# Forming the distance from the threshold to the largest score on VectorE, beside the selection, in a top-k attention and ELU kernel

## The chip, the cores and the metric

The kernel runs on one core of a Trainium2 chip. The metric is the device time of one execution in microseconds, from a median of several runs. The engines are named as in the profile: PE is the matrix engine (TensorE), PEld its weight loads, DVE is VectorE, ACT is ScalarE, POOL is GpSimd and SP issues DMAs.

## What is computed

The input is q, k and v with 8 batches, 8 heads, 576 rows and 64 columns, and two weights of an ELU layer. The reference, cut to what matters:

```python
scores = scale * np.matmul(q, k.transpose(0, 1, 3, 2))          # 576 x 576 for each head
kth = np.partition(scores, -top_k, axis=-1)[..., -top_k:-top_k + 1]   # top_k = 32
scores = np.where(scores >= kth, scores, -1000000000.0)
scores = scores - np.max(scores, axis=-1, keepdims=True)
attn = np.exp(scores)
attn = attn / (np.sum(attn, axis=-1, keepdims=True) + 1e-09)
o = np.matmul(attn, v)
# heads side by side: x is 4608 x 512
h = x @ w_in                                                    # 512 x 2048
g = np.where(h > 0.0, h, np.exp(np.minimum(h, 0.0)) - 1.0)
out = g @ w_out                                                 # 2048 x 512
```

Each row of scores needs its 32nd largest value (the threshold), its largest value, and the sum of exponentials over the kept scores. The kernel writes the exponential with a bias that is threshold minus largest score: this "gap" is one number for each row.

## The kernel before

**Steps.** The attention is cut into steps. A step is one tile of 128 query rows and two heads, so it handles two "score rows" of 128 partitions by 576 keys (index `i` is 0 or 1). There are 144 steps. In the first 8 (`n < tight`) the weights are still being decoded beside the selection and another form of it is used (`select_row`); three more use `select`; the last 133, from about 157 us on, use `select_folded`, and these are the ones the change touches.

**One step, by engine.** `scores` (L326) makes the scores on PE and ACT copies them from PSUM to SBUF (L343), two steps ahead. `select_folded` (L391) finds the 32nd largest on DVE: it folds a row of 576 into a row `high` of 288 maxima (L402), while POOL forms the 288 minima `low` in two integer operations (L403, L406). DVE takes the 32 largest of `high` by rounds of MAX8 and MATCH_REPLACE8 (L410 to L420), the 16 largest of `low` (L424 to L428), and joins the two lists (L430, L431). L430 writes the minima of pairs over places 15 to 30 of `found`, and L431 reduces them to the threshold, `u.last[:, i, 7]`. The largest score is `found[:, i, 0]`, left as it was by the join.

`mask(u, i)` (L436) belongs to the next step of the loop: for the previous tile, POOL forms the gap of one row (L453, one number for each partition), ACT sets what lies under the threshold far away (L454) and takes the exponential with the gap as its bias and the row sum as a by-product (L455 and the read of the accumulator behind it). `normalise` (L459) forms the reciprocal of the sums on POOL in five small operations (L465 to L470) and multiplies both rows by it (L472, two operations). One loop later `turn` (L476) transposes the rows on PE (L491), ACT copies them to SBUF (L492), and `attend` (L501) multiplies them by v on PE (L517) and copies the result to the layer's input (L544).

**The layer.** `ffn_pieces` (L565) gives pieces of the ELU layer: `hidden` (PE L589, three ACT operations L599, L602 and L604, and a DVE operation L561 that joins the two halves of the ELU, called a gate) and `project` (PE L614, ACT L623, output by DMA). `feed` (L702) places such pieces between the parts of a step, by costs and due times that are fixed when the program is built. So the order on each engine is written out at build time: the engines run it strictly in that order and wait for each other by semaphores.

**The order around the change.** With `cur` the step in selection and `prev` the one before, the loop (L743 to L797) issues in a folded step:

- DVE: L402, L410, rounds of L415 and L420, L424, L426, L428, L430, L431 for `cur`, with gates L561 in between
- POOL: L403 and L406 for `cur`, then L453 twice and L465 to L472 for `prev`
- ACT: L343 for a later step, then for `prev` L454 and L455 of row 0, pieces of the layer, L492 twice for the step before `prev`, L454 and L455 of row 1, pieces, L492 once more
- PE: scores of a later step, L517 of a finished group, pieces of the layer, transposes L491 in three portions with pieces in between

The tile `den` holds four numbers for each partition: two sums and two gaps. It comes from the pool `small`, with four buffers of each kind. `wk`, in which POOL writes `low`, has one buffer.

Of the kernel before, what the change touches and what calls it, by code (L numbers as in the profile page):

```python
# [9 lines left out]
ALU = mybir.AluOpType  # L10
AX = mybir.AxisListType
FP32 = mybir.dt.float32
# [13 lines left out]
class Tile:  # L26
# [6 lines left out]
    def __init__(self, b, qt, rows, block, cols):  # L33
        self.b, self.qt, self.rem = b, qt, qt == 4
        self.rows = rows
        self.block = block
        self.cols = cols
        self.ql = cols.stop - cols.start
# [21 lines left out]
class Step:  # L60
# [7 lines left out]
    def __init__(self, t, hp, group, at):  # L68
        self.t, self.hp = t, hp
        self.group, self.at = group, at  # L70
        self.masked = self.normal = self.turned = False
        if t.rem:
            rows = [(4 * hp, 0), (4 * hp + 2, 0), (4 * hp + 3, 1), (4 * hp + 1, 1)]
            self.heads = [
                (h, i, slice(64 * (n % 2), 64 * (n % 2) + 64))
                for n, (h, i) in enumerate(rows)
            ]
        else:
            self.heads = [(2 * hp + i, i, slice(0, 128)) for i in range(2)]
# [3 lines left out]
def kernel(  # L83
# [9 lines left out]
    nc = tc.nc  # L93
    P = nc.NUM_PARTITIONS
# [18 lines left out]
    def pool(name, bufs, **kw):  # L113
        return ctx.enter_context(tc.tile_pool(name=name, bufs=bufs, **kw))
# [6 lines left out]
    small = pool("small", 4)  # L121
# [269 lines left out]
    def select_folded(u):  # L391

        one, other = u.sc[:, :, 0:HS], u.sc[:, :, HS:S]
        high = late["high"].tile([P, 2, HS], FP32, tag="high", name="high")
        rest, low = (
            wk[:, i, :].rearrange("p (a s) -> p a s", a=2) for i in range(2)
        )
        found = late["top"].tile([P, 2, TOP_K], FP32, tag="found", name="found")
        second = late["top"].tile([P, 2, TOP_K // 2], FP32, tag="second", name="second")
        u.first = found  # L400
        u.last = small.tile([P, 2, 8], FP32, tag="m4", name="m4")
        nc.vector.tensor_tensor(high[:], one, other, ALU.max)  # L402
        nc.gpsimd.tensor_tensor(  # L403
            low.bitcast(I32), one.bitcast(I32), other.bitcast(I32), ALU.add
        )
        nc.gpsimd.tensor_tensor(  # L406
            low.bitcast(I32), low.bitcast(I32), high[:].bitcast(I32), ALU.subtract
        )
        for i in range(2):
            nc.vector.max(found[:, i, 0:8], high[:, i, :])  # L410
        yield
        cur = high
        for r in range(0, TOP_K - 8, 8):
            for i in range(2):
                nc.vector.match_replace(  # L415
                    rest[:, i, :], found[:, i, r : r + 8], cur[:, i, :], TAKEN
                )
            cur = rest
            for i in range(2):
                nc.vector.max(found[:, i, r + 8 : r + 16], rest[:, i, :])  # L420
            if r < TOP_K - 16:
                yield
        for i in range(2):
            nc.vector.max(second[:, i, 0:8], low[:, i, :])  # L424
        for i in range(2):
            nc.vector.match_replace(low[:, i, :], second[:, i, 0:8], low[:, i, :], TAKEN)  # L426
        for i in range(2):
            nc.vector.max(second[:, i, 8:16], low[:, i, :])  # L428
        pairs = found[:, :, TOP_K // 2 - 1 : TOP_K - 1]
        nc.vector.tensor_tensor(pairs, pairs, second[:, :, ::-1], ALU.min)  # L430
        nc.vector.tensor_reduce(  # L431
            u.last[:, :, 7:8], found[:, :, TOP_K // 2 - 1 : TOP_K], AX.X, ALU.max
        )
        yield

    def mask(u, i, early=False):  # L436

        if u.masked:
            return
        if i == 0:
            u.den = small.tile([P, 4], FP32, tag="den", name="den")
        u.masked = i == 1
        sc, low, top = u.sc[:, i, :], u.last[:, i, 7:8], u.first[:, i, 0:1]
        gap = u.den[:, 2 + i : 3 + i]
        if early:  # L450
            nc.scalar.activation(gap, top, AF.Prelu, scale=-1.0, bias=low, alpha=1.0)
        else:
            nc.gpsimd.tensor_tensor(gap, low, top, ALU.subtract)  # L453
        nc.scalar.activation(sc, sc, AF.Prelu, scale=-1.0, bias=low, alpha=1.0 / STEEP)  # L454
        nc.scalar.activation(  # L455
            sc, sc, AF.Exp, scale=-STEEP, bias=gap, accum_out=u.den[:, i : i + 1]
        )
# [285 lines left out]
    for n in range(NS + 3):  # L743
# [3 lines left out]
        if n < tight:  # L747
            turn_qk(True)
            if n < 3:
                scores(ahead)  # L750
            if n > 1:
                scores(step(n + 3))
            for i in range(2):
                passes = select_row(cur, i, n < tight - 1)
                next(passes)
                if i == 0:
                    while closing:
                        attend(closing.pop(0))
                elif prev:
                    normalise(prev)  # L760
                    turn(prev, main)
                    turn(prev, rest)
                    turn(prev, other)
                feed(n, 0.25)
                next(passes)
                mask(cur, i, True)
                feed(n, 0.25)
            continue
# [10 lines left out]
        if prev:  # L779
            mask(prev, 0)  # L780
# [6 lines left out]
        if prev:  # L787
            mask(prev, 1)
# [45 lines left out]
```

## Time and profile before

| | |
|---|---|
| median of 3 runs | 1723.7 us (1722.95 to 1725.91) |
| the profiled execution | 1726.9 us |
| its span, first to last instruction | 1725.1 us |
| PE busy | 1628.8 us, 94% of the span |
| DVE busy | 1456.8 us, 84% |
| ACT busy | 1099.1 us, 64% |
| POOL busy | 970.3 us, 56% |
| L453 on POOL, folded steps | 266 operations, 201 ns mean |
| L430 and L431 on DVE | 133 each, 192 and 191 ns mean |
| clock granted to PE | 0.97 of full speed, mean of the span |

The busy time of an engine is the time in which at least one of its instructions is in progress. A list of waits names the engine and line that sat idle, who ended the idle time, and then the microseconds in total, the number of waits and the longest one. In a timeline each row has the start, the duration, the engine, the line, the operation, its output and inputs, and in brackets the idle time of that engine before it with the one who ended it. A table of stretches gives, for each window of the span, the busy time of each engine with the number of instructions in brackets, then the granted clock of PE, the share of the DMA engines and the bandwidth.

### The profile page before, as it was taken

The numbers are of one execution on the slowest core, as the hardware profiler recorded it, in microseconds if no ns is written. First come the engines' busy times: TensorE is split into PE (matmuls) and PEld (weight loads), VectorE is DVE, ScalarE is ACT, GpSimd is POOL, SyncE is SP. The second block draws the span as 40 slices with busy tenths as digits, with TensorE's granted clock in tenths as the row PEclk, the third lists the DMA queues.
The fourth block names the chain that finished last, engine by engine and source line by source line (L and its number), as shares of the span: only waits on it lengthen the run. The fifth ranks groups of instructions, "written<-read, shape, count | busy, mean of one in ns | idle before, by whom it ended". The sixth has DMA issues, their size and how long they took to land.

```text
span 1725.1 us, 27135 instructions
## 1 busy us (share of the span) xinstructions
PE 1628.8 (94%) x8276; PEld 1029.4 (60%) x8276; DVE 1456.8 (84%) x4587; ACT 1099.1 (64%) x2305; POOL 970.3 (56%) x1681
## 2 busy tenths in 40 slices
PE   5789999999999999999999999999999999999999
PEld 3466667656565656555556565755557565755565
DVE  6978999998998998998988998889988898887600
ACT  6887666666575666666657565667657575666521
POOL 3765666665656566555655655556665556555400
PEclk8579999999999999999999999999999999999999
DMA  7431210012100210011200211002200101000000
GB/s 231 139 111 35 49 34 15 7 21 41 42 1 7 48 34 21 1 27 35 42 13 1 46 23 41 1 7 48 42 13 7 26 15 28 7 7 7 7 13 13
DMA packets 188050, 56.29 MB, mean 33 GB/s; under 512 B 178176, under 2 KB 179200, under 8 KB 187904
## 3 DMA queue, kind: packets, MB, share of 16 engines
q1 hardware_dynamic: 186704, 54.26, 13.5%
q8 instruction: 66, 1.08, 0.3%
q14 instruction: 80, 0.66, 0.1%
q10 hardware_dynamic: 1200, 0.30, 0.1%
HBM read 45.09 MB, written 9.44 MB: 32 GB/s over the span
## 4 chain that ended last, share of the span: by engine, by line
PE 30%; POOL 28%; ACT 21%; DVE 14%; issue 5%; DMA 1%; SPq 0%; POOLq 0%; DVEq 0%; ACTq 0%
PE ops L614 15%; POOL sc L472 7%; ACT sc L455 6%; POOL wk L406 6%; POOL wk L403 6%; PE hps L589 6%; PE avps L517 5%; ACT sc L454 4%; ACT et L492 4%; POOL rec L467 3%; DVE wk L415 3%; PE scps L335 2%; DVE found L420 2%; DVE second L424 2%; PE eps L491 2%
## 5 line engine op out<-in xcount | busy, mean ns | idle before, releaser
L589 PE MATMUL hps<-xT,w_in 128*128 128x256 f32 (+2 forms) x2432 | 548.1, 375 | 0.6 <-ACT gT L602 0.4
L614 PE MATMUL ops<-w_out,gT 128*128 128x512 f32 x1152 | 522.9, 598 | 0.0
L589 PEld LDWEIGHTS hps<-xT,w_in 128*128 128x128 f32 x2432 | 408.4, 194 | 101.8 <-issue 27.7
L455 ACT ACTIVATE sc<-sc,den 128x576 f32<-128x576 f32 x288 | 223.5, 776 | 352.5 <-POOL den L453 337.1
L465 POOL TENSOR_SCALAR dene<-den 128x2 f32<-128x2 f32 x144 | 37.7, 262 | 556.4 <-ACT sc L455 555.9
L614 PEld LDWEIGHTS ops<-w_out,gT 128*128 128x128 f32 x1152 | 208.9, 190 | 233.5 <-issue 213.5
L420 DVE MAX8 found<-wk 128x8 f32<-128x288 f32 x798 | 323.1, 446 | 0.0
L335 PE MATMUL scps<-kqT 64*128 64x288 f32 (+1 forms) x1280 | 226.3, 444 | 35.9 <-ACT et L492 23.3
L517 PE MATMUL avps<-et,vT 128*64 128x256 f32 (+2 forms) x2080 | 228.3, 337 | 30.8 <-ACT et L492 30.1
L472 POOL TENSOR_SCALAR sc<-sc,rec 128x576 f32<-128x576 f32 x288 | 233.6, 821 | 14.9 <-POOL rec L470 0.2
L415 DVE MATCH_REPLACE8 wk<-found,wk 128x288 f32<-128x288 f32 x532 | 231.2, 442 | 0.0
L454 ACT ACTIVATE sc<-sc,m 128x576 f32<-128x576 f32 x288 | 227.0, 788 | 0.0
L517 PEld LDWEIGHTS avps<-et,vT 128*64 128x64 f32 x2080 | 135.9, 145 | 125.0 <-ACT et L492 55.8
L561 DVE SCALAR_TENSOR_TENSOR gT<-n,gT 128x512 f32<-128x512 f32 (+1 forms) x156 | 112.5, 721 | 113.1 <-ACT n L604 113.1
L491 PEld LDWEIGHTS eps<-ident,sc 128*128 128x128 f32 x1152 | 145.1, 145 | 89.5 <-issue 49.7
L406 POOL TENSOR_TENSOR wk<-wk,high 128x576 int32<-128x576 int32 x133 | 190.7, 1434 | 10.4
L335 PEld LDWEIGHTS scps<-kqT 64*128 64x128 f32 (+1 forms) x1280 | 118.8, 182 | 124.9 <-issue 44.8
L491 PE MATMUL eps<-ident,sc 128*128 128x128 f32 x1152 | 177.5, 280 | 15.2 <-POOL sc L472 15.1
L343 ACT ACTIVATE sc<-scps 128x576 f32<-128x576 f32 x288 | 173.4, 657 | 28.9 <-PE scps L335 28.0
L403 POOL TENSOR_TENSOR wk<-sc 128x576 int32<-128x576 int32 x133 | 190.7, 1434 | 0.0
L424 DVE MAX8 second<-wk 128x8 f32<-128x288 f32 x266 | 108.3, 448 | 89.0 <-POOL wk L406 88.9
L492 ACT COPY et<-eps 128x512 f32<-128x512 f32 x288 | 164.8, 572 | 23.7 <-PE eps L491 23.7
(67 smaller groups left out, 1759.2 us busy)
## 6 DMA issues: line engine op xcount, KB each, us to landing
raw<-in_moe_w_in_dram SPq DMA_DIRECT2D x16, 512.0 KB, 5.8
vT<-in_v_dram SPq DMA_DIRECT2D x64, 128.0 KB, 2.4
raw<-in_moe_w_out_dram SPq DMA_DIRECT2D x16, 512.0 KB, 4.0
out_dram<-osb SPq DMA_DIRECT2D x32, 256.0 KB, 2.1
kin<-in_k_dram SPq DMA_DIRECT2D x112, 72.0 KB, 2.4
qin<-in_q_dram SPq DMA_DIRECT2D x112, 72.0 KB, 2.5
kin<-in_k_dram SPq DMA_DIRECT2D x8, 128.0 KB, 4.6
vT<-in_v_dram SPq DMA_DIRECT2D x64, 16.0 KB, 2.2
```

The costliest lines, as they stand in the source:

```text
L335: nc.tensor.matmul(wide[i][rows, half, 0:HS], kq[part, q0 : q0 + u.t.ql], kq[part, k0 : k0 + HS], start=True, stop=True,)
L403: nc.gpsimd.tensor_tensor(low.bitcast(I32), one.bitcast(I32), other.bitcast(I32), ALU.add)
L406: nc.gpsimd.tensor_tensor(low.bitcast(I32), low.bitcast(I32), high[:].bitcast(I32), ALU.subtract)
L415: nc.vector.match_replace(rest[:, i, :], found[:, i, r : r + 8], cur[:, i, :], TAKEN)
L420: nc.vector.max(found[:, i, r + 8 : r + 16], rest[:, i, :])
L454: nc.scalar.activation(sc, sc, AF.Prelu, scale=-1.0, bias=low, alpha=1.0 / STEEP)
L455: nc.scalar.activation(sc, sc, AF.Exp, scale=-STEEP, bias=gap, accum_out=u.den[:, i : i + 1])
L472: nc.gpsimd.tensor_scalar(u.sc[:, i, :], u.sc[:, i, :], rec[:, i : i + 1], 1.0, ALU.mult, ALU.mult)
L491: nc.tensor.transpose(ps[:, c * P : (c + 1) * P], sc[:, c0 : c0 + P], ident[:])
L517: nc.tensor.matmul(ps[i * D : (i + 1) * D, cols], vt[:, 2 * J + i if c == J else i * J + c, :], w, start=(c == 0), stop=(c == J),)
L589: nc.tensor.matmul(blk.h[:, f % bank, :], w_in[:, i, f * P : (f + 1) * P], blk.xT[:, i, 0:n_tok], start=(i == 0), stop=(i == NC - 1),)
L614: nc.tensor.matmul(blk.o[:], blk.gT[f // NG][:, f % NG, s * P : (s + 1) * P], w_out[:, f, :], start=(f == 0), stop=(f == NF - 1),)
```

## The change

In folded steps the gap is formed at the end of `select_folded`, on DVE, right behind the join: one operation on 128 partitions by 2 numbers covers both rows. `den` is therefore allocated there, one loop earlier than before. `mask` no longer forms the gap for such steps; the two POOL operations (L453) are not issued. Steps that are not folded keep what they had. The order of the PE and ACT queues is the same in both programs; DVE's has 133 operations more and POOL's 266 fewer.

```diff
@@ Step.__init__
-        self.masked = self.normal = self.turned = False
+        self.masked = self.normal = self.turned = self.spread = False
+        self.den = None
@@ select_folded
-        u.first = found
+        u.first, u.spread = found, True
...
         nc.vector.tensor_reduce(
             u.last[:, :, 7:8], found[:, :, TOP_K // 2 - 1 : TOP_K], AX.X, ALU.max
         )
+        u.den = small.tile([P, 4], FP32, tag="den", name="den")
+        nc.vector.tensor_tensor(
+            u.den[:, 2:4], u.last[:, :, 7], found[:, :, 0], ALU.subtract
+        )
         yield
@@ mask
-        if i == 0:
+        if u.den is None:
             u.den = small.tile([P, 4], FP32, tag="den", name="den")
...
-        else:
+        elif not u.spread:
             nc.gpsimd.tensor_tensor(gap, low, top, ALU.subtract)
```

## The prediction

> **What bounds the kernel now.** I read the list of waits first. Three of its rows form a ring:
>
> ```profile
> POOL dene L465 <- ACT sc L455: 555.9, 139, 10.8
> ACT sc L455 <- POOL den L453: 337.1, 106, 5.4
> DVE second L424 <- POOL wk L406: 88.9, 86, 2.0
> ```
>
> POOL waits for the exponentials, the exponentials wait for POOL's gap, and DVE waits for a POOL operation in front of that gap. The timeline of one step shows how, POOL first, then ACT:
>
> ```profile
> 899.79 0.23 POOL L465 TENSOR_SCALAR dene<-den 128x2 f32<-128x2 f32 x1 [4.47 <-ACT sc L455]
> ...
> 903.72 1.40 POOL L403 TENSOR_TENSOR wk<-sc 128x576 int32<-128x576 int32 x1
> 905.20 1.40 POOL L406 TENSOR_TENSOR wk<-wk,high 128x576 int32<-128x576 int32 x1
> 906.56 0.33 POOL L453 TENSOR_TENSOR den<-m,found 128x1 f32<-128x1 f32 x2
> 911.52 0.23 POOL L465 TENSOR_SCALAR dene<-den 128x2 f32<-128x2 f32 x1 [4.62 <-ACT sc L455]
> ```
>
> ```profile
> 902.61 0.80 ACT L454 ACTIVATE sc<-sc,m 128x576 f32<-128x576 f32 x1
> 906.78 0.78 ACT L455 ACTIVATE sc<-sc,den 128x576 f32<-128x576 f32 x1 [3.37 <-POOL den L453]
> ```
>
> The gap's inputs have been ready since the end of the selection before, some 9 us. L453 is late only because it stands in POOL's queue behind L403 and L406 of the next tile. POOL's 7.1 us (899.79 to 906.89) and ACT's 4.6 us (906.89 to 911.52) follow each other without a gap, and together they are the step: 11.73 us.
>
> But PE is 94% busy, and its order is fixed. So the second view is what PE itself waits for, from 180 us (the first folded steps) to 1660 us (the last attention product):
>
> ```profile
> PE avps L517 <- ACT et L492: 24.9, 45, 2.1
> PE scps L335 <- ACT et L492: 23.3, 27, 2.5
> PE eps L491 <- POOL sc L472: 0.9, 3, 0.5
> PE scps L491 <- POOL sc L472: 0.5, 1, 0.5
> ```
>
> 49.6 us in all. L492 stands in ACT's queue behind the held L455. The ring thus reaches the end of the program only through these stalls: behind 1660 us PE has a last block of the layer that needs all of the attention, and in the ring's longest steps PE still works nearly throughout. Third view, four of eight stretches:
>
> ```profile
> 180.00:300.00 120.00, 112.06 (x849) 79.08 (x851) 113.66 (x367) 77.63 (x166) 74.78 (x131) 0.97 0.18 35
> 300.00:500.00 200.00, 189.44 (x951) 123.12 (x948) 181.34 (x600) 126.33 (x263) 123.46 (x214) 0.98 0.12 24
> 500.00:700.00 200.00, 190.08 (x1054) 122.30 (x1054) 182.78 (x597) 129.73 (x270) 118.62 (x209) 0.99 0.12 24
> ...
> 900.00:1100.00 200.00, 195.17 (x1086) 129.08 (x1082) 178.30 (x581) 129.86 (x271) 115.83 (x206) 1.00 0.12 24
> ```
>
> The third number is PE's busy time, the fifth DVE's. Both are near the length of the stretch; no other engine is. What the ring gives back, PE or DVE limits soon.
>
> **What goes.** 266 L453 of 201 ns: 0.33 us a step of POOL, and with it ACT's wait in front of L455. In the folded part that wait is 335.6 us in 105 waits, 3.2 us each. Without it L455 of row 0 follows L454 at once (903.4 in place of 906.78), and row 1 must still wait for PE's transposes and two L492, so its end comes some 2 to 2.5 us sooner, and POOL's L465 with it. The ring is open: POOL's L403 and L406 no longer lie on ACT's path. What is late next is PE's own queue, or DVE.
>
> **What comes.** 133 DVE operations on 128x2. The nearest rows are L430 (192 ns) and L431 (191 ns), which start 0.22 us apart; behind L431 the next operation starts 0.11 us later. So 0.11 to 0.23 us a step; I take 0.22, 29 us of DVE in all. Behind it in DVE's queue stand a gate L561 or the next L402. ACT's L454 of that tile also needs L431 and comes about 5 us after it (909.48 against 914.62), so the longer wait costs ACT nothing. `den` with four buffers is held one loop longer, still two; no new wait.
>
> **What lies on the path, stage by stage.** A stretch can shrink to the larger of PE's busy time and DVE's with the new work. In every step DVE has at least 0.10 us of idle time that no wait explains, so I add 0.32 us for each folded step (12, 18, 19, 18, 18, 19, 18 and 10 of them start in the eight stretches).
> 180 to 300: DVE 113.66 + 3.8 = 117.5, above PE, so 2.5 us to gain. 300 to 500: DVE 187.1, PE 189.4: 10.6. 500 to 700: DVE 188.9, PE 190.1: 9.9. From there PE alone binds: 700 to 900, busy 193.5, gives 6.5; the next three, busy 195.2, 195.1 and 195.2, give 4.8, 4.9 and 4.8; 1500 to 1660, busy 158.3, gives 1.7. Sum: 45.7 us. This takes PE and DVE as free to drift within a stretch.
>
> They are not free. Cut at the starts of L402 and taking in each step the smaller of PE's idle time and DVE's (less 0.32, below nothing where DVE has less), the 133 steps yield 21 us. Over groups of three steps the same sum gives 33 us. Scores run two steps ahead and transposes one to two steps behind, so three steps are nearest to what the queues allow: I take **33 us**, and keep 21 and 46 as ends.
>
> **The clock.** After 180 us the granted clock falls to half in short stretches, for instance
>
> ```profile
> 385.50:389.00 3.50, 3.50 (x15) 1.76 (x12) 2.69 (x9) 0.59 (x2) 3.42 (x4) 0.51 0.00 0
> ```
>
> Here the 18 products L517 take 3.92 us in place of 2.37. There are five such stretches of 3.4 us and one of 6.8, 24 us in all, so about 12 us of PE time lost; all six come within 3 us of a PE stall on L492 of 1.2 to 2.5 us. PE's busy time above contains the loss. Nothing says how many return; between 0 and 12 I take 6.
>
> Sum: 33 + 6 = 39 us off the profiled execution, 1726.9 to 1688. That execution lies 3.2 us above the median of the runs, so in their terms 1723.7 - 39 = **1685 us**.
>
> **A rule that speaks against it.** DVE's L561 takes 683 ns in the middle, but 1.31 us at 324.10, where POOL's L406 (323.44, 1.42 us) is under way. L402 takes 0.75, but 1.24 us at 215.08 beside L472. DVE operations with two inputs in SBUF are thus stretched to the end of a POOL operation that runs already. The Trainium skill ("SBUF — State Buffer", "Who interferes with whom") says the same of a shared pair of ports: the one who issues second is fully blocked until the first finishes. The new operation is of this kind, and by the rule alone each could cost up to the 1.4 us of an L403, or 186 us of DVE if all 133 were met. By the rows, L430, of the same kind at the same place, never exceeded 194 ns in 133 cases, since POOL is then waiting for L455; but POOL will come 2 us earlier against DVE, and then L402 may be met more often. I leave this out of the sum and give it to the rivals.
>
> **Rivals.**
>
> *DVE or the shared port takes most of it.* For: at 180 to 700 us DVE has hardly more slack than PE, and 17 of the 67 steps there show DVE idle for 0.10 us only. Against: from 700 us DVE has over 1 us a step free. Without the clock's 6 us, the tight pairing of 21 us less one stretched L402 (0.49 us) in every fourth of those 67 steps (8 us) leaves 13: 1711 us. Range 1702 to 1716. Chance 0.22.
>
> *The stalls stay.* PE's waits may be the plain handing over of transposes through ACT (0.30 us in many cases), and ACT then waits for PE where it waited for POOL. For: after L453 the next waits of ACT are for PE (L544 60.3, L623 59.9 us). Against: in those steps L492 runs straight behind L455's accumulator read, so it was ready before. Then within 0.2%: 1723. Chance 0.07.
>
> *Slower.* Port collisions in most steps: L402 stretched by 0.49, a gate by 0.5 (1.1 a step), the new 0.22, 1.26 us of DVE a step. DVE's waits in the folded part, 88.9 us for L406 and 39.0 for L604, are 0.96 us a step; beyond that point DVE sets the pace and each 0.1 us costs 13 us. All steps: 0.30 x 133 = 40 us, 1764. Against: POOL is idle 4 to 5 us in each step, and DVE waits behind L406, which holds the two in phase. Chance 0.08.
>
> **The numbers.** Forecast 0.63, its own range 1666 (46 and 12 us) to 1702 (21, none); rivals 0.22, 0.07, 0.08. The range takes in forecast and first rival, 0.85: 1666 to 1716. A measurement of this kernel can tell about 0.2%, 3.4 us, from no change. Faster 0.85, same 0.07, slower 0.08.
>
> **What would show it.** Right: the wait of L455 on L453 gone and that of L465 shorter, PE's waits on L492 from 48 to under 15 us, fewer half-clock stretches, the wait of L424 on L406 smaller, DVE's L436 at about 0.19 us, L402 at 0.75. Wrong: PE idle as long as before, or PE waiting for POOL's L472 or DVE's gates; L402 or L561 longer in many steps; L455 waiting for DVE.

## The result and the profile after

The changed kernel takes 1729.5 us (median of 13 runs, 1727.6 to 1732.0) beside 1725.9 us before (13 runs, 1723.0 to 1727.0): a ratio of 1.0025, 95% interval 1.0017 to 1.0034. It is slightly slower, where 1685 was forecast. Its profiled execution has a span of 1726.1 us.

The page's busy times and the engine shares of the chain that ended last, of the changed kernel:

```profile
PE 1624.8 (94%) x8276; PEld 1033.9 (60%) x8276; DVE 1580.4 (92%) x4720; ACT 1114.2 (65%) x2305; POOL 896.8 (52%) x1415
...
DVE 79%; PE 12%; ACT 3%; issue 2%; POOL 2%; DMA 1%; SPq 0%; DVEq 0%; POOLq 0%; ACTq 0%
```

DVE was busy for 1456.8 us before; now it is 1580.4, and 79% of the chain is DVE. (Line numbers are larger by one up to the join, so the fold L402 is now L403 and the reduction L431 is L432; the new operation is L436; from `mask` on they are larger by five, so L454 and L455 are L459 and L460, and L492 is L497. Each experiment has its own lines again.)

Five rows of the list of waits of the changed kernel:

```profile
POOL dene L470 <- ACT sc L460: 288.1, 139, 11.2
ACT sc L459 <- DVE m L432: 246.0, 95, 6.0
POOL wk L404 <- DVE second L429: 220.8, 120, 5.1
...
POOL wk L407 <- DVE high L403: 131.6, 122, 2.8
...
ACT sc L460 <- DVE den L436: 29.1, 97, 0.4
```

The ring of before is open: the exponential's wait of 337.1 us for POOL's gap is gone, and POOL's wait for the exponential fell from 555.9 to 288.1. But the waits did not vanish. ACT and POOL now run ahead until they meet DVE. The third row is the one to remember: POOL's first low operation (L404, before L403) never waited for DVE before: it started 4.4 us behind the start of the fold, in the median. Now it waits in 120 of 133 steps for L429, DVE's last reader of the single buffer `wk`, and starts 1.4 us ahead of the fold.

What POOL does when it is let go is seen in the groups of DVE, with busy time, mean duration in ns and idle time before:

```profile
L436 DVE TENSOR_TENSOR den<-m,found 128x2 f32<-128x2 f32 x133 | 130.0, 977 | 4.5
L403 DVE TENSOR_TENSOR high<-sc 128x576 f32<-128x576 f32 x133 | 99.1, 745 | 5.0 <-PE ops L619 5.0
```

and in the timeline of one step, first DVE, then POOL:

```profile
972.16 0.81 DVE L429 MAX8 second<-wk 128x8 f32<-128x288 f32 x2
973.00 0.19 DVE L431 TENSOR_TENSOR found<-found,second 128x32 f32<-128x32 f32 x1
973.23 0.19 DVE L432 TENSOR_REDUCE m<-found 128x2 f32<-128x34 f32 x1
973.46 1.03 DVE L436 TENSOR_TENSOR den<-m,found 128x2 f32<-128x2 f32 x1
974.41 0.75 DVE L403 TENSOR_TENSOR high<-sc 128x576 f32<-128x576 f32 x1
```

```profile
973.05 1.41 POOL L404 TENSOR_TENSOR wk<-sc 128x576 int32<-128x576 int32 x1 [1.65 <-DVE second L429]
975.30 1.41 POOL L407 TENSOR_TENSOR wk<-wk,high 128x576 int32<-128x576 int32 x1 [0.83 <-DVE high L403]
```

An operation on two numbers for each partition takes 1.03 us. It ends at 974.49, when POOL's L404 ends (974.46). POOL is released at the end of L429 (972.97), starts beside L431, and is under way when L436 comes up. In 122 of the 133 steps L436 meets L404 like this. A DVE step without gates now takes 10.05 us with 0.14 us of idle time; before, such a step had about 9.0 us of work, and DVE waited another 1.03 us in it for L406. So the wait that the open ring took away came back as a longer operation.

Two stretches of the changed kernel show who paces (third number PE's busy time, fifth DVE's):

```profile
500.00:700.00 200.00, 189.17 (x1028) 121.78 (x1027) 197.41 (x606) 129.25 (x264) 110.08 (x171) 0.96 0.12 24
...
1300.00:1500.00 200.00, 196.24 (x1104) 131.51 (x1103) 197.54 (x613) 136.45 (x281) 107.49 (x174) 0.99 0.07 17
```

DVE has 197.5 of the 200 us in both.

### The profile page after: what moved, and what is told of

Its sections match the earlier page's. It is cut to its first block, busy times and chain, and to the rows that moved or that the text cites. A ratio compares the mean times of both kernels' runs of the same rounds, so it can differ in the third digit from the quotient of the medians.

```text
span 1726.1 us, 27110 instructions
## 1 busy us (share of the span) xinstructions
PE 1624.8 (94%) x8276; PEld 1033.9 (60%) x8276; DVE 1580.4 (92%) x4720; ACT 1114.2 (65%) x2305; POOL 896.8 (52%) x1415
## 4 chain that ended last, share of the span: by engine, by line
DVE 79%; PE 12%; ACT 3%; issue 2%; POOL 2%; DMA 1%; SPq 0%; DVEq 0%; POOLq 0%; ACTq 0%
DVE wk L416 18%; DVE found L421 15%; DVE den L436 7%; DVE wk L427 6%; DVE second L429 5%; DVE found L411 5%; DVE second L425 5%; DVE gT L566 5%; DVE high L403 5%; PE ops L619 5%; PE hps L594 4%; DVE kqT L290 2%; DVE found L431 2%; DVE m L432 1%; PE avps L522 1%
## 5 line engine op out<-in xcount | busy, mean ns | idle before, releaser
L459 ACT ACTIVATE sc<-sc,m 128x576 f32<-128x576 f32 x288 | 225.4, 783 | 246.5 <-DVE m L432 246.0
L404 POOL TENSOR_TENSOR wk<-sc 128x576 int32<-128x576 int32 x133 | 187.9, 1413 | 220.8 <-DVE second L429 220.8
L336 PE MATMUL scps<-kqT 64*128 64x288 f32 (+1 forms) x1280 | 221.6, 450 | 43.5 <-ACT et L497 30.8
L460 ACT ACTIVATE sc<-sc,den 128x576 f32<-128x576 f32 x288 | 223.4, 776 | 35.2 <-DVE den L436 29.1
L477 POOL TENSOR_SCALAR sc<-sc,rec 128x576 f32<-128x576 f32 x288 | 217.1, 764 | 15.0 <-POOL rec L475 0.2
L522 PEld LDWEIGHTS avps<-et,vT 128*64 128x64 f32 x2080 | 140.7, 151 | 112.9 <-ACT et L497 40.4
L497 ACT COPY et<-eps 128x512 f32<-128x512 f32 x288 | 164.8, 572 | 40.5 <-PE eps L496 39.8
L566 DVE SCALAR_TENSOR_TENSOR gT<-n,gT 128x512 f32<-128x512 f32 (+1 forms) x156 | 118.1, 758 | 74.8 <-ACT n L609 74.8
L470 POOL TENSOR_SCALAR dene<-den 128x2 f32<-128x2 f32 x144 | 34.5, 240 | 288.5 <-ACT sc L460 288.1
L604 ACT ACTIVATE n<-hps 128x512 f32<-128x512 f32 (+1 forms) x156 | 86.9, 557 | 75.1 <-PE hps L594 47.8
```

The costliest lines, as they stand in the source:

```text
L336: nc.tensor.matmul(wide[i][rows, half, 0:HS], kq[part, q0 : q0 + u.t.ql], kq[part, k0 : k0 + HS], start=True, stop=True,)
L460: nc.scalar.activation(sc, sc, AF.Exp, scale=-STEEP, bias=gap, accum_out=u.den[:, i : i + 1])
L477: nc.gpsimd.tensor_scalar(u.sc[:, i, :], u.sc[:, i, :], rec[:, i : i + 1], 1.0, ALU.mult, ALU.mult)
L522: nc.tensor.matmul(ps[i * D : (i + 1) * D, cols], vt[:, 2 * J + i if c == J else i * J + c, :], w, start=(c == 0), stop=(c == J),)
L566: nc.vector.scalar_tensor_tensor(out=dst, in0=n, scalar=-1.0, in1=dst, op0=ALU.add, op1=ALU.add)
```

## The experiments

The theory, called LOCK: a POOL operation that reads SBUF and is under way holds up a DVE operation with two SBUF inputs until it ends; and in the opened ring POOL's first low operation, released by DVE's own L429, always stands in front of the first such DVE operation behind the join. The rivals: OWN COST (the new operation is dear by itself, being strided and fed by the reduction right before it) and FULL (DVE had no room for one more operation, however short).

**1. The gap on ACT.** DVE's new operation is removed; ACT forms the gap, as the early steps do.

```diff
-        u.den = small.tile([P, 4], FP32, tag="den", name="den")
-        nc.vector.tensor_tensor(
-            u.den[:, 2:4], u.last[:, :, 7], found[:, :, 0], ALU.subtract
-        )
...
-        if early:
+        if early or u.spread:
             nc.scalar.activation(gap, top, AF.Prelu, scale=-1.0, bias=low, alpha=1.0)
-        elif not u.spread:
+        else:
```

> The gap is formed by ACT in folded steps (two Prelu operations of 0.3 us a step, as the early steps do it); neither POOL nor DVE has an operation for it. Theory LOCK: in the changed kernel POOL's first low operation (1.41 us) is released by DVE's last MAX8 of the step before, starts while DVE does the two operations of the join, and blocks the first DVE operation behind them that has two SBUF inputs. Without the new operation that is the fold (high, two inputs), which then takes about 1.7 us in place of 0.75; the DVE step stays near 10.0 us and the time within 0.5% of the changed kernel, 1722 to 1735. Theory OWN COST (the new operation takes 1.03 us by itself): without it the DVE step falls by 0.95 us, the fold stays at 0.75, and PE paces: 1680 to 1700. Theory FULL (DVE simply has no room for one more operation): same, 1680 to 1700.

Measured: 1721.9 us, 0.9980 of before (0.9968 to 0.9992), 0.1 us under LOCK's range. The fold and the longer of the gates, of this kernel's DVE groups:

```profile
L403 DVE TENSOR_TENSOR high<-sc 128x576 f32<-128x576 f32 x133 | 177.4, 1334 | 4.8 <-PE ops L615 4.8
L562 DVE SCALAR_TENSOR_TENSOR gT<-n,gT 128x512 f32<-128x512 f32 x108 | 118.1, 1093 | 73.6 <-ACT n L605 73.3 <-issue 0.2
```

The fold's median is 1.74 us, its mean 1.33, since it is not always the fold that pays: it comes up behind L404 in 75 steps, and a gate that stands ahead of it in 45 more (the longer gates took 732 ns in the mean before). With the new operation gone, the next one in line with two SBUF inputs pays: OWN COST and FULL are wrong, and opening the ring without any new DVE work brings only 0.2%. A step of it, DVE and then POOL:

```profile
966.67 0.19 DVE L432 TENSOR_REDUCE m<-found 128x2 f32<-128x34 f32 x1
966.77 1.74 DVE L403 TENSOR_TENSOR high<-sc 128x576 f32<-128x576 f32 x1
```

```profile
966.49 1.41 POOL L404 TENSOR_TENSOR wk<-sc 128x576 int32<-128x576 int32 x1 [1.13 <-DVE second L429]
```

POOL's operation ends at 966.49 + 1.41 = 967.90, and the fold ends 0.6 us later, at 968.51: most of its 0.75 us of work came only then.

**2. The DVE operation alone.** The kernel before keeps POOL's gap, and the new operation is added at the same place, with its result written where nothing reads it.

```diff
+        nc.vector.tensor_tensor(
+            second[:, :, 0], u.last[:, :, 7], found[:, :, 0], ALU.subtract
+        )
         yield
```

> The kernel before, with POOL's gap kept, and the new DVE operation added at the same place with its result thrown away. LOCK: POOL still comes late, its low operations start 5 us behind the fold, so the added operation takes 0.16 to 0.19 us and lies in DVE's idle time: 0 to 5 us slower than before. OWN COST: the added operation takes 1.0 us here too, and the time rises by 10 to 60 us. FULL: the added operation is short and the time rises by 5 to 29 us (0.22 us x 133).

Measured: 1732.1 us, 1.0038 of before (1.0025 to 1.0050), so 5.3 us slower, just above LOCK's range and at the lower edge of FULL's. The operation has a median of 163 ns and a mean of 171:

```profile
L434 DVE TENSOR_TENSOR second<-m,found 128x2 f32<-128x2 f32 x133 | 22.8, 171 | 4.5
```

By itself it costs 0.16 us, so OWN COST is wrong; FULL is not excluded by this run alone. DVE was busy 34.1 us longer than before (1490.9 beside 1456.8), 22.8 of it this operation and 13.5 its gates; its wait for L406 fell from 88.9 to 72.9 us and paid for about half. In the changed kernel the same operation has 130.0 us in all, so 130.0 - 133 x 0.163 = 108 us are blocking.

**3. The low operations behind the fold.** The changed kernel, with POOL's two integer operations in the other order. The sum is the same, but the first now reads the fold's output.

```diff
         nc.gpsimd.tensor_tensor(
-            low.bitcast(I32), one.bitcast(I32), other.bitcast(I32), ALU.add
+            low.bitcast(I32), one.bitcast(I32), high[:].bitcast(I32), ALU.subtract
         )
         nc.gpsimd.tensor_tensor(
-            low.bitcast(I32), low.bitcast(I32), high[:].bitcast(I32), ALU.subtract
+            low.bitcast(I32), low.bitcast(I32), other.bitcast(I32), ALU.add
         )
```

> The changed kernel, with POOL's two integer operations in the other order: first one minus high, then plus other. The same numbers come out, but the first of them now needs the fold and starts behind it. LOCK: the new operation falls from 1.03 to under 0.2 us, the fold stays at 0.75, the DVE step without gates falls from 10.05 to about 9.3 us, and PE paces again: 1680 to 1705. OWN COST: the new operation stays at 1.03 us and the time within 0.5% of the changed kernel. FULL: the new operation is short, but the time stays above 1715.

Measured: 1651.2 us, 0.9570 of before (0.9557 to 0.9583). Its DVE groups:

```profile
L403 DVE TENSOR_TENSOR high<-sc 128x576 f32<-128x576 f32 x133 | 99.6, 749 | 3.1 <-PE ops L619 3.1
...
L436 DVE TENSOR_TENSOR den<-m,found 128x2 f32<-128x2 f32 x133 | 25.4, 191 | 4.5
```

The same DVE operation at the same place falls from 130.0 to 25.4 us, the fold stays short, and the time falls below LOCK's range of 1680 to 1705. This shows what held the new operation; the size of what it frees was too small in my forecast as well (see below).

**4. Two operations with one tensor input each.** In the changed kernel the second operand becomes one number for each partition.

```diff
-        nc.vector.tensor_tensor(
-            u.den[:, 2:4], u.last[:, :, 7], found[:, :, 0], ALU.subtract
-        )
+        for i in range(2):
+            nc.vector.tensor_scalar(
+                u.den[:, 2 + i : 3 + i], u.last[:, i, 7:8], found[:, i, 0:1], None,
+                ALU.subtract,
+            )
```

> The changed kernel with two operations of one SBUF tensor input each (the second operand is one number for each partition) in place of the one with two tensor inputs. LOCK: each takes about 0.19 us or less, but the fold behind them now takes about 1.4 us and the DVE step stays near 10 us: time within 0.5% of the changed kernel. OWN COST (of two strided tensor inputs): the two take 0.4 us in place of 1.03, the fold stays at 0.75, and the time falls to 1680 to 1705. FULL: time like the changed kernel or 5 to 15 us slower, with no operation stretched.

Measured: 1721.3 us, 0.9966 of before (0.9957 to 0.9975). Against the changed kernel's 1.0025 that is 0.6% less, just outside LOCK's 0.5%, and far from the 1680 to 1705 of OWN COST. The two take 202 to 216 ns each, all 266 of them, with L404 under way beside 246 (the other 20 take 202 to 215); the fold behind them pays, in 78 steps, or a gate ahead of it, in 46:

```profile
L403 DVE TENSOR_TENSOR high<-sc 128x576 f32<-128x576 f32 x133 | 149.7, 1126 | 4.9 <-PE ops L621 4.9
...
L437 DVE TENSOR_SCALAR den<-m,found 128x1 f32<-128x1 f32 x266 | 44.5, 209 | 4.7
```

So it is the operation with a second SBUF tensor that is blocked, not any operation at that place.

**5. Control: the other order in the kernel before.** The edit of experiment 3 alone.

> Control: the kernel before, with POOL's two integer operations in the other order and nothing else. LOCK: in the kernel before POOL reaches these operations some 5 us behind the fold, so the new dependency costs and brings nothing: within 0.4% of before, 1719 to 1734, and ACT still waits some 330 us for POOL's gap. Rival SWAP (the 4% of the earlier run come from the order itself, by better reads or fewer collisions with gates): 1650 to 1690.

Measured: 1726.1 us, 0.9999 of before (0.9989 to 1.0008), and ACT's wait for the gap is 335.9 us (335.6 before). The order by itself is worth nothing; it counts only where the ring is open.

**6. The gap on ACT and the other order.** Experiments 1 and 3 together.

> The gap on ACT, as before, and POOL's two integer operations in the other order. LOCK: with POOL's first low operation behind the fold, the fold falls from 1.33 us mean to 0.75, and DVE saves the new operation besides (0.2 us a step): 1635 to 1660, not slower than the changed kernel with the other order (1651). If ACT's 0.6 us a step lie on the path: 1660 to 1690. If the fold stays above 1.2 us: LOCK is wrong, about 1720.

Measured: 1644.8 us, 0.9527 of before (0.9513 to 0.9542). The fold's mean is 779 ns. Against experiment 3 that is 6 us less: DVE's one new operation costs more than ACT's two.

**7. The gap first in POOL's queue.** It stays on POOL, as one operation for both rows, but ahead of the two low operations, which keep the old order. DVE has nothing new.

```diff
+    def gaps(u):
+        u.den = small.tile([P, 4], FP32, tag="den", name="den")
+        nc.gpsimd.tensor_tensor(
+            u.den[:, 2:4], u.last[:, :, 7], u.first[:, :, 0], ALU.subtract
+        )
...
             attend(closing.pop(0))
+        if prev and prev.spread:
+            gaps(prev)
         next(passes)
```

> The gap stays on POOL (one operation for both rows), but stands in POOL's queue ahead of the two low operations, in the old order; DVE has no new operation. ACT need not wait for the low operations either, so the ring is open. LOCK: POOL's gap is released by the reduction at the end of the join, so the low operation comes about 0.3 us later than in the changed kernel, just behind the start of the fold, which then wins: fold near 0.75, low operation behind it, 1640 to 1670. Rival PHASE (an open ring always puts POOL's first low operation in front of the fold): fold at 1.2 to 1.7 us, 1710 to 1725. Rival DVE-MUST (only moving the gap off POOL opens the ring): ACT's wait for the gap stays, 1715 to 1727.

Measured: 1631.6 us, 0.9442 of before (0.9426 to 0.9458), a little below LOCK's range and the fastest kernel of this study. POOL and then DVE in one step of it:

```profile
962.51 0.50 POOL L439 TENSOR_TENSOR den<-m,found 128x2 f32<-128x2 f32 x1 [1.15 <-DVE m L432]
962.97 1.93 POOL L404 TENSOR_TENSOR wk<-sc 128x576 int32<-128x576 int32 x1
```

```profile
962.28 0.68 DVE L568 SCALAR_TENSOR_TENSOR gT<-n,gT 128x512 f32<-128x512 f32 x1
962.88 0.75 DVE L403 TENSOR_TENSOR high<-sc 128x576 f32<-128x576 f32 x1
```

Now the two sides are exchanged. POOL's gap is released by the reduction, which ends 0.45 us after L429, and here DVE's gate and fold are in front: POOL's gap takes 0.50 us in place of 0.20 and its low operation 1.93 in place of 1.41, where POOL has time. It goes like this in 26 of the 133 steps. In 57 the gap is held beside the fold (0.63 us in the median) and the low operation starts right behind the fold; in 45 it starts later still, and in 5 ahead of the fold. The fold has a mean of 775 ns, so the rival PHASE is wrong: an open ring does not always put POOL first.

**8. Experiments 7 and 3 together.**

> The run above with POOL's two integer operations in the other order as well. LOCK: the low operations are behind the fold in any case; within 0.5% of the run above if that one had no collisions left, 1640 to 1665; clearly faster than it if it had. PHASE: 1640 to 1665 here alone.

Measured: 1636.8 us, 0.9479 of before (0.9464 to 0.9494). That is 0.3% above experiment 7, within the 0.5% given, though 3 us under the stated 1640. The fold's mean is 784 ns beside 775 there, so the other order had nothing left to take off the fold. Where the 5 us come from was not taken apart.

## Why the prediction was wrong

**What bounds the kernel: the ring, right.** Opening it without putting a blocked operation in DVE's queue gives 4.3 to 5.6% (experiments 3, 6 and 7).

**What goes: right as far as it went, but what is late next was missed.** The step said that POOL's L465 comes 2 to 2.5 us sooner and that PE or DVE is late next. It did not follow POOL to the next thing that holds it: its first low operation writes `wk`, of which there is one buffer, and L429 is the last reader. POOL ran ahead exactly to that wait (220.8 us in 120 waits), and from there on its start is tied to DVE's own instructions. The prediction had POOL come 2 us earlier against DVE; its first low operation came 5.8 us earlier against the fold, in the median, and so from behind it to ahead of it.

**What comes: the step that failed.** I priced the new operation at 0.22 us from L430 and L431, its neighbours, in DVE's groups before:

```profile
L430 DVE TENSOR_TENSOR found<-found,second 128x32 f32<-128x32 f32 x133 | 25.6, 192 | 4.5
L431 DVE TENSOR_REDUCE m<-found 128x2 f32<-128x34 f32 x133 | 25.4, 191 | 4.5
```

L431 is a reduction, and no reduction was held up in any run. L430 has two SBUF inputs and was short because no large POOL operation was under way beside it: POOL was idle in 117 of its 133 cases and in the others busy with operations on 128x2. The prediction itself says so for most ("since POOL is then waiting for L455"), and that idle time is what the change takes away. The measured price is 0.98 us in the mean, 130 us in all where 29 were put into the sum. ACT's wait for DVE, priced at nothing from a slack of 5 us, became 246.0 us, since ACT no longer lost that slack in front of the exponential.

**The rule that speaks against it: left out of the sum, and it was the answer.** The Trainium skill's rule ("SBUF — State Buffer", "Who interferes with whom") names a DVE operation with two SBUF inputs beside a GpSimd operation that reads SBUF, and says that a `tensor_reduce` never contends. The trace agrees on both: beside the same L404, L432 takes 190 to 196 ns and L436 1.03 us. It does not bear the rule out for small POOL operations, which held up nothing (last section); there the measurement decides. By the rule I had worked out 186 us if all 133 new operations were met; 122 were, and 108 us were lost. But I gave the collisions to the two rivals at 0.22 and 0.08, as hits of the fold and the gates, and left the new operation at 0.22 us in both. The second rival's case against ("POOL is idle 4 to 5 us in each step, and DVE waits behind L406, which holds the two in phase") rested on phases of the old ring. The new phase was not a matter of chance: POOL's release (L429) stands two DVE operations ahead of L436.

**Stage by stage: the floor of PE was put too high.** By PE's busy time I allowed 46 us at most, and 12 more from the clock. Experiment 3, the same change without the blocking of its new operation, takes 76 us off before, and experiment 7 takes 95. PE's busy time is not its work alone. Of the kernel before, one step:

```profile
908.80 0.75 PE L335 MATMUL scps<-kqT 64*128 64x288 f32 x2
909.84 1.23 PE L335 MATMUL scps<-kqT 64*128 64x288 f32 x6 [0.29 <-ACT et L492]
911.00 0.65 PE L517 MATMUL avps<-et,vT 128*64 128x256 f32 x2
911.95 2.37 PE L517 MATMUL avps<-et,vT 128*64 128x256 f32 x18 [0.30 <-ACT et L492]
```

The eight score products count 1.98 us of busy time when a stall splits them, and 1.24 us in one piece (972.48 in experiment 3). A stall of 0.29 us thus costs about 1 us, of which the profile calls 0.7 busy. Before, 27 of 154 such groups of eight are split by a stall, in experiment 7 only 6. With the same 8276 products, PE's busy time is 1628.8 us before and 1572.5 in experiment 7; score and attention products of the widest forms account for 18.5 and 26.6 us of it (203.3 to 184.8, 169.7 to 143.1). PE's idle time in the span fell from 96.3 to 58.4 us besides. How much of the busy time was the half clock was not taken apart.

**The clock: not as forecast, as the stalls stayed.** PE's waits on the copies L497, between 180 and 1660 us, are 47.5 us in the changed kernel (48.2 before), in fewer and longer waits, and its half-clock stretches there rose from 24 to 61 us. In experiment 3 both fell, to 18.4 and 7 us (less a stretch at the very end of the program).

**A slip in the working.** The 67 steps that the first rival puts at 180 to 700 us run to 900 us; 49 start by 700, and 13 of them show DVE idle for 0.10 to 0.12 us. That moves the rival's 1711 us by about 2 and explains nothing of the miss.

Of the forecast's own signs, "DVE's L436 at about 0.19 us" was the one that told at once; of the signs of being wrong, "L455 waiting for DVE" came (29.1 us in 97 waits), while L402 stayed at 0.75 us.

## What to carry to other kernels

When a change takes a wait out of a ring, follow the freed engine to the next wait in its queue and ask whose instruction ends it: if it is another engine's, the two are then in step, and what collides once collides nearly every time (here in 122 of 133 steps). A duration read beside an idle engine is a price only as long as that engine stays idle; before pricing a VectorE operation with two SBUF inputs by a short neighbour, see what GpSimd will be doing at that place after the change. And where a queue holds up a cheap operation, its place in the queue may be all that has to change: moved ahead on POOL, as one operation for both rows, it beat moving the work to DVE or ACT (1631.6 us beside 1651.2 and 1644.8, the best time of each).

## What the hardware showed beyond that

- Blocking works both ways and goes by who starts first: L436 is stretched from 0.16 to 1.03 us by a POOL operation under way, and POOL's low operation from 1.41 to 1.93 us by a fold under way. A DVE operation that reads one tensor and one number for each partition (202 to 216 ns) is not touched, nor is a reduction (190 to 196 ns).
- A small POOL operation under way holds nothing up. Before, L430 came up nine times behind L467, which works on 128x2 and had 0.22 to 0.43 us of its 0.72 us to run; L430 took 191 to 194 ns. In all ten traces together, from 170 us on, a DVE operation with two SBUF inputs came up 278 times at least 0.1 us behind the start of a POOL operation on 128x2 that ran for another 0.1 us, and none was lengthened by 0.05 us. Behind POOL operations on 128x576, 894 of 948 were lengthened by more than 0.09 us. Why the small ones hold nothing up was not tested.
- In the kernel before, half-clock stretches of 3.4 us come without any PE idle time above 2.5 us: after stalls of 1.2 to 2.5 us, at 225, 280, 341, 386 and 604 us, and one of 6.8 us at 799 us. The length of the stall alone does not decide: four others of 1.5 to 1.8 us (at 496, 581, 691 and 1200 us) had no such stretch behind them.
